# Scores and states of the second batch: two separate steps in the gaps between MLP units, in place of one block inside a unit's output products

## The chip, the cores and the metric

One core of a Trainium2 chip runs the whole kernel. The metric is the device time of one execution in microseconds. The kernel before took 1019.85 us (median of three runs, 1019.58 to 1019.98).

## The reference

All tensors are fp32. A retention layer without softmax (8 batches, 8 heads, 576 tokens, head size 64) is followed by a two-layer MLP over 4608 tokens, with a leaky ReLU of a learned slope for each of the 2048 hidden channels:

```python
scores = scale * np.matmul(q, k.transpose(0, 1, 3, 2))
gamma = 1.0 - 2.0 ** (-5.0 - np.arange(H, dtype=np.float32))
Dmat = np.where(rel >= 0, gamma[:, None, None] ** rel[None, :, :], 0.0)
ret = np.matmul(scores * Dmat[None, :, :, :], v)

h = x @ w_in                                  # x: (4608, 512), w_in: (512, 2048)
g = np.maximum(h, 0.0) + alpha * np.minimum(h, 0.0)
return g @ w_out                              # w_out: (2048, 512)
```

## The kernel before

**Attention in chunks.** Two heads make a pair; each batch has four pairs, numbered through, so the second batch is pairs 4 to 7. From the second batch on, a pair is worked in nine chunks of 64 tokens. Four things happen to it:

- its operands are prepared: `scale_pair` (step "p": GpSimd scales `qx` in L534, ScalarE scales `vn` in L539) and `transposes` (step "t": two 32x32 block transposes on VectorE, L545);
- scores of each chunk, `k q^T`, by 18 small matmuls, which VectorE scales and masks into `mt`, while ScalarE copies `qT` into the other half of `mt`;
- states of the first eight chunks, `k^T v`, by 16 small matmuls, which `running_sums` (step "u") adds up with the decay: one ScalarE copy (L556), then six VectorE instructions (L558, L562, L564); `pair_sums` (step "w", L570) copies the sums to `vn` on ScalarE;
- values (step "v"): 36 small matmuls of `vn` with `mt` (L630), ScalarE copies of the result into the MLP's input `xb` (L641), and the loads of the pair after next on SP's queue.

**The MLP.** From the third block of 256 tokens on (`mlp_unit`), each unit of 2 x 128 hidden channels is a Strassen-like product with seven multiplications instead of eight, from combined weights. The first two blocks (`PLAIN`) use plain products while the weights are still arriving. A plain unit is `plain_unit` (8 instructions, in the trace 16 matmuls of 256 columns, into `ph`, L429, then two ScalarE activations, L433 and L435), `plain_relu` (two VectorE instructions, L445, that read `ph` and make `g`), and one unit later `mlp_out`, which calls `plain_out` (4 instructions, in the trace 8 matmuls of 512 columns, L408). `ph` lies in one PSUM bank with the tag `psh0`, of which there is one, so a unit's first matmul follows the relu of the unit before. The names `ps`, `pu` and `pv` are tiles of the tag `psa`, of which there are two.

**Weights.** Each piece of a weight (512 KB) is loaded into a ring, split by ScalarE (`piece_in`, L299 and L301) and rounded by three VectorE instructions (`piece_out`, L310, L313, L315) and one of GpSimd (L317), which also fetches the piece six ahead. `combine` makes the weights' sums on GpSimd (L327).

**The order.** The part up to `ordered.close()` is written out by hand: each engine executes in the order in which the program calls. Every engine runs its own instructions in order and waits for the others by semaphores. The change acts on the last loop of this part: twelve plain units, here unit 0 to unit 11, with at most two pieces in each. The steps of pairs 4 to 7 are hung into it by two tables, `before` (behind the relu, ahead of the products) and `after` (behind the products and the second `piece_in`). Pair n's scores and states come together in `pair_front`: `amid` is called from within `mlp_out`, ahead of its last product, in units 2, 4, 7 and 9. The ninth chunk's scores have a PSUM tile of their own there, `pe`, with the tag `psh0`, and the masks of that chunk are two VectorE instructions (L607), beside four of 256 columns (L614). The other eight chunks share two `psa` tiles with the states.

```python
        if n in fronts:
            mlp_out((3, lambda: amid(fronts[n])))
            piece_out(1)
        else:
            piece_out(1)
            mlp_out()
```

After the loop the blocks of the other batches follow, with `joint` doing the attention of pairs 8 to 31 between the MLP units; there values and scores share tiles, and `pair_front` stays in use.

Of the kernel before, what the change touches and what calls it, by code (L numbers as in the profile page):

```python
# [18 lines left out]
def kernel(  # L19
# [380 lines left out]
    def plain_out(kb, i, g, between):  # L400
        if i == 0:
            acc[kb] = [ps_o.tile([P, DM], FP32, tag=f"pso{2 * kb + m}", name=f"po{m}_{kb}")
                       for m in range(2)]
        for x in range(2):
            for m in range(2):
                if between and 2 * x + m == between[0]:
                    between[1]()
                nc.tensor.matmul(acc[kb][m], g[:, 2 * x + m],  # L408
                                 w_out[i][:, 2 * x:2 * x + 2].rearrange("p x f -> p (x f)"),
                                 start=(i == 0 and x == 0), stop=(i == NU - 1 and x == 1))  # L410
        if i == NU - 1:
            po = acc.pop(kb)
            osb = ring.tile([P, 2, DM], FP32, tag=f"o{kb}", name=f"osb_{kb}")
            for m in range(2):
                t0 = kb * TB + m * P
                nc.scalar.copy(osb[:, m], po[m])
                nc.sync.dma_start(out[t0:t0 + P, :], osb[:, m])
        if kb == PLAIN[-1] and i % UST == UST - 1:
            waiting.extend((w_in[i // UST], x) for x in S_WORK)
            waiting.extend((w_out[j], x) for j in range(i + 1 - UST, i + 1) for x in T_WORK)  # L420
# [127 lines left out]
    def chunk(j):  # L548
        return slice(j * C, (j + 1) * C)

    def running_sums(n, even, odd):
        c = pairs[n][1]
        su = attn.tile([P, S], FP32, tag="kT", name=f"su_{n}")[:, 0:S - D].rearrange(
            "p (j d) -> p j d", d=D)
        g1, g2 = gch[:, 0, c:c + 1], gch[:, 1, c:c + 1]
        nc.scalar.copy(su[:, 0::2], even)  # L556
        for h2 in range(2):
            nc.vector.scalar_tensor_tensor(  # L558
                out=su[half(h2), 1::2], in0=su[half(h2), 0::2], scalar=g1[half(h2)],
                in1=odd[half(1 - h2)], op0=ALU.mult, op1=ALU.add)  # L560
        for j in range(3, NJ - 1, 2):
            nc.vector.scalar_tensor_tensor(out=su[:, j], in0=su[:, j - 2], scalar=g2,  # L562
                                           in1=su[:, j], op0=ALU.mult, op1=ALU.add)
        nc.vector.scalar_tensor_tensor(out=su[:, 2::2], in0=su[:, 1:NJ - 3:2], scalar=g1,  # L564
                                       in1=even[:, 1:], op0=ALU.mult, op1=ALU.add)
        return su
# [4 lines left out]

    later = []

    def last_chunk(n, extra):
        kT, qT = turned[n]
        for h2 in range(2):  # L580
            nc.tensor.matmul(extra[half(1 - h2)], kT[half(h2), chunk(NJ - 1)],  # L581
                             qT[half(h2), chunk(NJ - 1)], start=True, stop=True)

    def pair_front(n, kT, qT, kn, vn, extra):

        c = pairs[n][1]
        mts[n] = mt = attn.tile([P, 2 * S], FP32, tag="at", name=f"mt_{n}").rearrange(
            "p (h j s) -> p h j s", h=2, s=C)
        assert C == D and NJ == 9
        ps = [ps_tile([P, 2, NM - 1, C], f"ps{p2}_{n}") for p2 in range(2)]  # L590
        for j in range(NJ - 1):
            for h2 in range(2):
                x = half((1 - h2, h2)[j % 2])
                nc.tensor.matmul(ps[j % 2][x, 0, j // 2],  # L594
                                 kT[half(h2), chunk(j)], qT[half(h2), chunk(j)],
                                 start=True, stop=True, skip_group_check=True)
        for j in range(NJ - 1):
            for h2 in range(2):
                x = half((h2, 1 - h2)[j % 2])
                nc.tensor.matmul(ps[j % 2][x, 1, j // 2], kn[half(1 - h2), j],  # L600
                                 vn[half(1 - h2), h2, j], start=True, stop=True,
                                 skip_group_check=True)
        for h2 in range(2):
            nc.scalar.copy(mt[half(h2), h2].rearrange("p j s -> p (j s)"), qT[half(h2)])
        for h2 in range(2):
            to = half(1 - h2)
            nc.vector.scalar_tensor_tensor(  # L607
                out=mt[to, h2, NJ - 1], in0=extra[to],
                scalar=th[to, 3, 2 * c + h2:2 * c + h2 + 1], in1=mask(to),
                op0=ALU.mult, op1=ALU.mult)  # L610
        for p2 in range(2):
            for h2 in range(2):
                h, to, x = 2 * c + h2, half(1 - h2), (1 - h2, h2)[p2]
                nc.vector.scalar_tensor_tensor(  # L614
                    out=mt[to, h2, p2:NJ - 1:2], in0=ps[p2][half(x), 0],
                    scalar=th[to, 3, h:h + 1],
                    in1=mask(to)[:, None, :].to_broadcast([C, NM - 1, C]),
                    op0=ALU.mult, op1=ALU.mult)
        later.append(lambda: running_sums(n, ps[0][:, 1], ps[1][:, 1]))

    def pair_values(n, vn, mt, pv=None, then=None):
        b, c = pairs[n]
# [214 lines left out]
    part_scale(1, 2)  # L837
    part_transposes(1, 0)
    piece_in(1)
    mlp_out((2, lambda: part_transposes(1, 1)))  # L840
    piece_out(1)
    piece_in(1)
    banks = part_scores(1)
# [38 lines left out]
    def step(what, n):  # L882
        if what == "p":
            scale_pair(n)
        elif what == "t":
            if n > last:
                combine_x(len(PLAIN))
            turned[n] = transposes(n)
        elif what == "u":
            sus[n] = later.pop(0)()  # L890
        elif what == "w":
            pair_sums(loaded[n][3], sus.pop(n))
        elif what == "v":
            pair_values(n, loaded[n][3], mts[n])
            del loaded[n]
            loaded[n + 2] = load_pair(n + 2)

    def amid(n):  # L900
        extra = ps_h.tile([P, C], FP32, tag="psh0", name=f"pe_{n}")
        last_chunk(n, extra)
        pair_front(n, *turned.pop(n), loaded[n][0], loaded[n][3], extra)

    last = 2 * NPAIR - 1
    before, after, fronts = {1: (("t", NPAIR),)}, {0: (("p", NPAIR),)}, {}
    for n, at in zip(range(NPAIR, last + 1), (2, 4, 7, 9)):
        fronts[at] = n  # L910
        after[at] = (("u", n),)
        before[at + 1] = (("w", n), ("p", n + 1))
        after[at + 1] = (("v", n), ("t", n + 1))

    units = [(kb, i) for i in range(UST, NU) for kb in PLAIN]
    for n, (kb, i) in enumerate(units):
        plain_unit(kb, i)
        plain_relu()
        for x in before.pop(n, ()):
            step(*x)  # L920
        piece_in(1)
        if n in fronts:
            mlp_out((3, lambda: amid(fronts[n])))
            piece_out(1)
        else:
            piece_out(1)
            mlp_out()
        combine(1)
        piece_in(1)
        for x in after.pop(n, ()):  # L930
            step(*x)
        piece_out(1)
        combine(2)
    assert not before and not after
    ordered.close()
    tc.no_sync_barrier()
    enqueue(0)
# [8 lines left out]
    def joint(n):  # L946
        pv = [ps_h.tile([P, 8, C], FP32, tag=f"psh{m}", name=f"pv{m}_{n}") for m in range(2)]


        extra = pv[1][:, 7]  # L950

        def chunk_8():
            if n < len(pairs):
                last_chunk(n, extra)

        if n - 1 in mts:
            pair_values(n - 1, loaded.pop(n - 1)[3], mts.pop(n - 1), pv, chunk_8)
        else:
            chunk_8()
        if n == len(pairs):  # L960
            return
        pair_front(n, *turned.pop(n), loaded[n][0], loaded[n][3], extra)
        if n + 1 < len(pairs):
            if n + 1 not in loaded:
                loaded[n + 1] = load_pair(n + 1)
            later.append(lambda: operands(n + 1))
# [3 lines left out]
    for b in range(2, B):  # L970


        nq = len(queue)
        at = [u + (u % NU == 0) for u in (c * nq // NPAIR + 2 for c in range(NPAIR))]
        if b == 2:
            at = [0, 3] + at[1:]
        for u in range(nq):
            first = queue[0][1] == 0
            pop_units(1)
            if later and not first:  # L980
                su = later.pop(0)()
                if su is not None:
                    pair_sums(loaded[n - 1][3], su)
            if u in at:
                assert not later
                joint(n)
                n += 1
        enqueue(b)
# [32 lines left out]
```

## Time and profile before

| | |
|---|---|
| median of three runs | 1019.85 us |
| time of the profiled execution | 1019.85 us |
| span of the profiled execution, first to last instruction | 1018.1 us |
| granted TensorE clock, mean | 0.999 |
| busy: PE, PEld, DVE, ACT, POOL | 1002.7, 898.6, 774.0, 266.2, 179.7 us |
| the twelve plain units of the loop | from 60.67 to 161.21 us |

PE is TensorE's matmul, PEld its weight load, DVE is VectorE, ACT ScalarE, POOL GpSimd, SP the engine that issues most of the loads. Times within the profile count from the first instruction. The ends of matmuls are modelled, so the start of the next instruction is the better mark of when PE went on. In a line of the timeline the columns are start, duration, engine, source line, operation, tiles and shapes; a bracket behind it gives the idle time of the engine ahead of it and what ended it. In the table of waits they are the total, the number of waits and the longest, in us. Matmuls in fp32 appear twice in the trace for one instruction of the program.

### The profile page before, as it was taken

What the parts mean: (1) busy time and instruction counts of PE and PEld (TensorE: products, weight loads), DVE (VectorE), ACT (ScalarE), POOL (GpSimd) and SP (SyncE); (2) the same over time, 40 slices, a digit from 0 to 9 for tenths busy, and PEclk for the clock granted to TensorE, in tenths of its full rate; (3) what the DMA queues carried; (4) which work ended last, traced back from release to release, by engine and by line L of the source; (5) the groups of instructions that cost most, each with busy time, mean ns of one, the idle gap of its engine ahead of it and who ended that gap; (6) DMA issues with size and microseconds to landing.
All of it is one profiled execution on the core that took longest, in us unless ns stands there. A gap on an engine that the chain in (4) does not pass through costs nothing.

```text
span 1018.1 us, 22392 instructions
## 1 busy us (share of the span) xinstructions
PE 1002.7 (98%) x9023; PEld 898.6 (88%) x9023; DVE 774.0 (76%) x2094; ACT 266.2 (26%) x602; POOL 179.7 (18%) x200
## 2 busy tenths in 40 slices
PE   7999999999999999999999999999999999999998
PEld 6766667999999999999999999999999999999997
DVE  6668895987787878786877787877778786667665
ACT  4556654222222222021121222222222210000000
POOL 5646664400100020100001000200020001010000
PEclk9999999999999999999999999999999999999999
DMA  9964754332232323121220232322222000000000
GB/s 242 246 176 123 170 104 100 61 73 54 42 69 39 66 48 69 18 53 34 51 47 23 46 69 48 69 48 63 54 42 51 14 22 1 22 1 22 1 22 22
DMA packets 229592, 64.25 MB, mean 63 GB/s; under 512 B 214368, under 2 KB 223088, under 8 KB 229488
## 3 DMA queue, kind: packets, MB, share of 16 engines
q1 hardware_dynamic: 227088, 62.02, 27.0%
q8 instruction: 71, 1.16, 0.5%
q10 hardware_dynamic: 2400, 0.79, 0.4%
q14 instruction: 33, 0.27, 0.1%
HBM read 53.35 MB, written 9.44 MB: 62 GB/s over the span
## 4 chain that ended last, share of the span: by engine, by line
PE 84%; DVE 0%; ACT 0%; DVEq 0%; issue 0%; ACTq 0%
PE ph L473 40%; PE po L391 38%; PE pv L630 3%; PE ps L594 1%; PE ps L600 1%; PE po L408 1%; PE pv L581 1%; PE ph L429 0%; ACT vn L570 0%; DVE s L370 0%; DVE u L370 0%; DVE osb L371 0%; DVEq L1016 0%; DVE osb L370 0%; ACTq L570 0%
## 5 line engine op out<-in xcount | busy, mean ns | idle before, releaser
L391 PE MATMUL po<-w_out,g 128*128 128x256 f32 x1792 | 408.1, 379 | 0.0
L391 PEld LDWEIGHTS po<-w_out,g 128*128 128x128 f32 x1792 | 330.7, 190 | 39.7
L484 DVE TENSOR_TENSOR g<-ph,g 128x256 f32<-128x256 f32 (+1 forms) x512 | 187.6, 387 | 136.4 <-PE ph L473 68.5
L473 PE MATMUL ph<-xb,w_in 128*128 128x128 f32 x2048 | 272.7, 276 | 0.0
L473 PEld LDWEIGHTS ph<-xb,w_in 128*128 128x128 f32 x2048 | 257.1, 192 | 7.4 <-issue 0.5
L473 PE MATMUL ph<-xt,w_in 128*128 128x128 f32 x1536 | 213.3, 275 | 0.0
L473 PEld LDWEIGHTS ph<-xt,w_in 128*128 128x128 f32 x1536 | 192.1, 192 | 0.0
L479 ACT COPY g<-ph 128x128 f32<-128x128 f32 x128 | 34.0, 265 | 404.1 <-PE ph L473 391.7
L495 DVE TENSOR_TENSOR g<-g 128x128 f32<-128x128 f32 x512 | 127.9, 291 | 7.0
L534 POOL TENSOR_TENSOR qx<-qx,tabx 128x576 f32<-128x576 f32 x28 | 32.8, 1170 | 355.1 <-DMA qx<-in_q_dram 276.5
L489 DVE SCALAR_TENSOR_TENSOR g<-g 128x512 f32<-128x512 f32 x128 | 90.0, 703 | 3.1
L487 DVE TENSOR_SCALAR g<-g,alpha 128x256 f32<-128x256 f32 x256 | 85.0, 374 | 3.6
L429 PE MATMUL ph<-xb,w_in 128*128 128x256 f32 x256 | 58.4, 382 | 2.1 <-DVE g L445 2.1
L408 PE MATMUL po<-w_out,g 128*128 128x512 f32 x128 | 59.1, 598 | 0.9 <-DVE g L445 0.9
L429 PEld LDWEIGHTS ph<-xb,w_in 128*128 128x128 f32 x256 | 48.0, 190 | 12.7 <-issue 4.0
L614 DVE SCALAR_TENSOR_TENSOR mt<-ps,th,mask 64x256 f32<-64x256 f32 x112 | 54.1, 483 | 3.9 <-PE ps L600 1.5
L641 ACT COPY xb<-pv 128x256 f32<-128x256 f32 (+3 forms) x84 | 23.1, 315 | 126.5 <-PE pv L630 126.5
L570 ACT COPY vn<-su 64x512 f32<-64x512 f32 x56 | 34.5, 617 | 80.1 <-DVE su L564 79.7
L459 POOL TENSOR_TENSOR xt<-xb 128x256 f32<-128x256 f32 x16 | 11.7, 728 | 196.5 <-PE ph L473 196.5
L607 DVE SCALAR_TENSOR_TENSOR mt<-pv,th,mask 64x64 f32<-64x64 f32 x48 | 13.6, 283 | 40.0 <-ACT xb L641 39.7
L630 PEld LDWEIGHTS pv<-mt,vn 128*64 128x64 f32 x1008 | 32.6, 138 | 12.9 <-DVE g L495 7.6
L539 ACT ACTIVATE vn<-vn,tabv 64x576 f32<-64x576 f32 x56 | 43.3, 772 | 1.7 <-DMA vn<-in_v_dram 0.5
(129 smaller groups left out, 742.6 us busy)
## 6 DMA issues: line engine op xcount, KB each, us to landing
out_dram<-osb SPq DMA_DIRECT2D x34, 256.0 KB, 2.1
kx<-in_k_dram SPq DMA_DIRECT2D x112, 72.0 KB, 2.7
qx<-in_q_dram SPq DMA_DIRECT2D x112, 72.0 KB, 2.9
vn<-in_v_dram SPq DMA_DIRECT2D x56, 144.0 KB, 3.4
kn<-in_k_dram SPq DMA_DIRECT2D x56, 144.0 KB, 3.7
raw<-in_moe_w_in_dram SPq DMA_DIRECT2D x24, 256.0 KB, 4.0
raw<-in_moe_w_out_dram SPq DMA_DIRECT2D x10, 512.0 KB, 5.1
w_in<-in_moe_w_out_dram SPq DMA_DIRECT2D x6, 512.0 KB, 4.6
```

Source lines behind the costliest of these rows:

```text
L391: nc.tensor.matmul(acc[kb][n // 2][:, n % 2, :], g[:, x, :], w_out[i][:, y, :], start=(i == 0 and n % 2 == 0), stop=(i == NU - 1 and (n % ...
L408: nc.tensor.matmul(acc[kb][m], g[:, 2 * x + m], w_out[i][:, 2 * x:2 * x + 2].rearrange("p x f -> p (x f)"), start=(i == 0 and x == 0), sto ...
L429: nc.tensor.matmul(ph[:, x], w_in[i // UST][:, cc // 2 * 2 + x, i % UST, cc % 2], xb[kb][:, cc], start=(cc == 0 and x == 0), stop=(cc == N ...
L473: nc.tensor.matmul(ph[m][:, o], w_in[i // UST][:, l, i % UST, cc], r[:, cc], start=(n in (0, 3) and cc == 0), stop=(n in (2, 6) and cc == ...
L484: nc.vector.tensor_tensor(out=o, in0=x0, in1=x1, op=ALU.add)
L487: nc.vector.tensor_scalar(g[:, 4 + 2 * m:6 + 2 * m], g[:, 2 * m:2 * m + 2], 0.0, alpha[:, fc:fc + 1], ALU.min, ALU.mult)
L489: nc.vector.scalar_tensor_tensor(out=g[:, 0:4].rearrange("p x t -> p (x t)"), in0=g[:, 0:4].rearrange("p x t -> p (x t)"), scalar=0.0, in1 ...
L495: ins = nc.vector.tensor_tensor(out=g[:, o, :], in0=g[:, x0, :], in1=g[:, x1, :], op=op)
L539: nc.scalar.activation(vn[x, h2], vn[x, h2], ACTF.Copy, scale=tabv[x, c:c + 1])
L570: nc.scalar.copy(vn[half(h2), h2, 1:], su[half(h2)])
L614: nc.vector.scalar_tensor_tensor(out=mt[to, h2, p2:NJ - 1:2], in0=ps[p2][half(x), 0], scalar=th[to, 3, h:h + 1], in1=mask(to)[:, None, :]. ...
L630: nc.tensor.matmul(pv[j >= j1][half(h2), j - (j1 if j >= j1 else 0)], vn[:, h2, j], mt[:, h2, j], start=True, stop=True)
```

## The change

The block of scores and states is taken out of the middle of the output products, and becomes two steps of their own, "s" (`pair_scores`) and "u" (`pair_states`, which ends with the running sums). All nine chunks' scores go to two `psa` tiles of up to five chunks, so `pe` and its two mask instructions go, and the four masks cover nine chunks (two of 320 columns, two of 256). States have two `psa` tiles of their own. The steps are worked off from one list, one entry in each gap; from unit 2 on a unit has two gaps, A behind the relu and ahead of the products, B behind the products and the second `piece_in`:

| pair | scores | states and sums | sums to `vn`, next pair's scaling | values, next pair's transposes |
|---|---|---|---|---|
| 4, before | 2, inside products | 2 (sums in B) | 3 A | 3 B |
| 4, after | 2 A | 2 B | 3 A | 3 B |
| 5, before | 4, inside products | 4 (sums in B) | 5 A | 5 B |
| 5, after | 4 B | 5 A | 5 B | 6 A |
| 6, before | 7, inside products | 7 (sums in B) | 8 A | 8 B |
| 6, after | 7 A | 7 B | 8 A | 8 B |
| 7, before | 9, inside products | 9 (sums in B) | 10 A | 10 B |
| 7, after | 9 B | 10 A | 10 B | 11 A |

The third step ("w", "p") is in gap A before, and in pairs 5 and 7 in gap B after. The combination of the third block's input, `combine_x(2)`, moves with the transposes of pair 8. In unit 0 the scaling of pair 4 moves ahead of the second piece. The number of matmuls stays; VectorE has eight instructions fewer. Code outside the loop is the same but for a few lines that pass the running sums on, and its order stays.

```diff
+    def pair_scores(n, kT, qT):
+        c = pairs[n][1]
+        mt = attn.tile([P, 2 * S], FP32, tag="at", name=f"mt_{n}").rearrange(
+            "p (h j s) -> p h j s", h=2, s=C)
+        ps = [ps_tile([P, NM, C], f"ps{p2}_{n}") for p2 in range(2)]
+        for j in range(NJ):
+            for h2 in range(2):
+                x = (1 - h2, h2)[j % 2]
+                nc.tensor.matmul(ps[j % 2][half(x), j // 2], kT[half(h2), chunk(j)],
+                                 qT[half(h2), chunk(j)], start=True, stop=True)
+        for h2 in range(2):
+            nc.scalar.copy(mt[half(h2), h2].rearrange("p j s -> p (j s)"), qT[half(h2)])
+        for p2 in range(2):
+            for h2 in range(2):
+                h, to, x = 2 * c + h2, half(1 - h2), (1 - h2, h2)[p2]
+                nm = NM - p2
+                nc.vector.scalar_tensor_tensor(
+                    out=mt[to, h2, p2::2], in0=ps[p2][half(x), 0:nm], scalar=th[to, 3, h:h + 1],
+                    in1=mask(to)[:, None, :].to_broadcast([C, nm, C]), op0=ALU.mult, op1=ALU.mult)
+        return mt
+
+    def pair_states(n, kn, vn):
+        ps = [ps_tile([P, NM - 1, D], f"pu{p2}_{n}") for p2 in range(2)]
+        for j in range(NJ - 1):
+            for h2 in range(2):
+                x = (h2, 1 - h2)[j % 2]
+                nc.tensor.matmul(ps[j % 2][half(x), j // 2], kn[half(1 - h2), j],
+                                 vn[half(1 - h2), h2, j], start=True, stop=True)
+        return running_sums(n, *ps)
...
     def step(what, n):
...
+        elif what == "s":
+            mts[n] = pair_scores(n, *turned.pop(n))
         elif what == "u":
-            sus[n] = later.pop(0)()
+            sus[n] = pair_states(n, loaded[n][0], loaded[n][3])
...
-    def amid(n):
-        extra = ps_h.tile([P, C], FP32, tag="psh0", name=f"pe_{n}")
-        last_chunk(n, extra)
-        pair_front(n, *turned.pop(n), loaded[n][0], loaded[n][3], extra)
-
     last = 2 * NPAIR - 1
-    before, after, fronts = {1: (("t", NPAIR),)}, {0: (("p", NPAIR),)}, {}
-    for n, at in zip(range(NPAIR, last + 1), (2, 4, 7, 9)):
-        fronts[at] = n
-        after[at] = (("u", n),)
-        before[at + 1] = (("w", n), ("p", n + 1))
-        after[at + 1] = (("v", n), ("t", n + 1))
+    steps = [(("t", NPAIR),)]
+    for n in range(NPAIR, last + 1):
+        steps += [(("s", n),), (("u", n),), (("w", n), ("p", n + 1)), (("v", n), ("t", n + 1)), ()]
+
+    def gap():
+        for x in steps.pop(0) if steps else ():
+            if x == ("t", last + 1):
+                combine_x(len(PLAIN))
+            step(*x)
...
         plain_unit(kb, i)
         plain_relu()
-        for x in before.pop(n, ()):
-            step(*x)
+        if n >= 1:
+            gap()
         piece_in(1)
-        if n in fronts:
-            mlp_out((3, lambda: amid(fronts[n])))
-            piece_out(1)
-        else:
-            piece_out(1)
-            mlp_out()
+        piece_out(1)
+        mlp_out()
+        if n == 0:
+            step("p", NPAIR)
         combine(1)
         piece_in(1)
-        for x in after.pop(n, ()):
-            step(*x)
+        if n >= 2:
+            gap()
         piece_out(1)
         combine(2)
```

## The prediction

> **What bounds the kernel now.** I read the page first, then busy time by stretches, the waits of TensorE, and the timelines of PE and DVE where the change acts. The page's engine row:
>
> ```profile
> PE 1002.7 (98%) x9023; PEld 898.6 (88%) x9023; DVE 774.0 (76%) x2094; ACT 266.2 (26%) x602; POOL 179.7 (18%) x200
> ```
>
> PE is busy for 98% of the span, so a change pays only where PE idles. The twelve plain units of the loop run from 60.67 (first `ph`, L429) to 161.21 (first L473). The stretches are units 0-1, 2-6, 7-11 and the rest:
>
> ```profile
> 60.67:74.44 13.77, 13.77 (x49) 9.12 (x48) 7.07 (x12) 8.14 (x14) 7.20 (x6) 1.00 0.77 185
> 74.44:118.35 43.91, 41.19 (x329) 27.30 (x328) 38.09 (x70) 27.97 (x55) 27.71 (x27) 1.00 0.51 142
> 118.35:161.21 42.86, 41.09 (x329) 27.55 (x330) 32.08 (x59) 22.50 (x45) 31.12 (x35) 1.00 0.57 114
> ```
>
> After the range come its length and the busy time of PE, PEld, DVE, ACT and POOL. Units 0-1 have no idle PE: 6.885 us a unit. In units 2-11 PE idles 2.72 + 1.77 = 4.49 us, with DVE at 38.09 of 43.91. Behind 161.21 PE waits for nothing that the trace lists. What PE waits for inside:
>
> ```profile
> PE ph L429 <- DVE g L445: 2.1, 4, 0.8
> PE pe L581 <- DVE g L445: 1.3, 2, 0.7
> PE pv L630 <- ACT vn L570: 1.0, 3, 0.4
> ```
>
> So a unit's `ph` (or the `pe` tile, in the same PSUM buffer) waits for DVE's late relu of the unit before. Pair 4, PE and then DVE:
>
> ```profile
> 74.44 3.62 PE L429 MATMUL ph<-xb,w_in 128*128 128x256 f32 x16
> 77.90 2.74 PE L408 MATMUL po<-w_out,g 128*128 128x512 f32 x6
> 80.56 0.27 PE L581 MATMUL pe<-qT,kT 64*64 64x64 f32 x2
> ...
> 81.76 1.13 PE L408 MATMUL po<-w_out,g 128*128 128x512 f32 x2
> 82.72 3.62 PE L429 MATMUL ph<-xb,w_in 128*128 128x256 f32 x16
> 86.17 3.60 PE L408 MATMUL po<-w_out,g 128*128 128x512 f32 x8
> 89.70 1.61 PE L630 MATMUL pv<-mt,vn 128*64 128x64 f32 x36
> 91.75 3.69 PE L429 MATMUL ph<-xb,w_in 128*128 128x256 f32 x16 [0.45 <-DVE g L445]
> ```
>
> ```profile
> 79.22 0.87 DVE L445 SCALAR_TENSOR_TENSOR g<-g,nalpha,ph 128x256 f32<-128x256 f32 x2 [0.36 <-ACT ph L435]
> 80.94 0.58 DVE L607 SCALAR_TENSOR_TENSOR mt<-pe,th,mask 64x64 f32<-64x64 f32 x2 [0.86 <-PE pe L581]
> 81.89 1.99 DVE L614 SCALAR_TENSOR_TENSOR mt<-ps,th,mask 64x256 f32<-64x256 f32 x4 [0.36 <-PE ps L600]
> 83.80 0.68 DVE L310 TENSOR_SCALAR wc<-wa 128x512 f32<-128x512 f32 x1
> ...
> 85.97 0.98 DVE L558 SCALAR_TENSOR_TENSOR su<-su,gch,ps 64x256 f32<-64x256 f32 x2
> ...
> 88.68 0.69 DVE L310 TENSOR_SCALAR wc<-wa 128x512 f32<-128x512 f32 x1
> ...
> 90.74 0.86 DVE L445 SCALAR_TENSOR_TENSOR g<-g,nalpha,ph 128x256 f32<-128x256 f32 x2
> ```
>
> DVE stands still 1.2 us for the front, which PE reaches only after six of eight `po` matmuls. Masks, a weight piece, running sums and a second piece follow in order. The next relu starts at 90.74 though ACT had finished near 87.5, and `ph` starts 1.01 us after the relu's start.
>
> **The change, part by part.** (a) *Scores leave the middle of the products.* For pairs 4 and 6 they stand before `mlp_out`, straight after `ph`, so they are ready (77.90 + 0.75) before the relu ends (80.0). DVE's 0.86 and 0.36 go. (b) *Six mask instructions become four.* The chunk 8 mask (283 ns, twice) goes; two of four grow from 256 to 320 columns, which no row shows. It costs at least the 256-column row, 483 ns, at most that plus a 64-column row, 766; the line through both rows gives 550, nearest to the 256 row, which I take. A mask set is 2 x 0.55 + 2 x 0.48 = 2.05 us, where relu's end to piece took 83.80 - 80.0 = 3.8: DVE is 1.75 earlier. Between the bounds, 1.9 to 1.3.
>
> (c) *Pairs 5 and 7 are spread.* Scores go after unit 4's products, states after unit 5's `ph`, values after unit 6's `ph`, not after unit 5's products (7 likewise in 9 to 11). The relu of unit 5 then has only a mask set and a piece ahead of it, and sums fall behind it. (d) *`pe` goes*, and with it its wait for the relu.
>
> Walk units 2-6 with rows of the trace: relu 0.8, a piece 2.06 (88.68 to 90.74), sums 2.7 (85.97 to 88.68), transposes 1.35, `ph` 3.45, products 3.45. Masks end at 82.05, piece 84.1, sums 86.8, piece 88.9: relu 3 runs 88.9-89.7. PE: scores to 78.65, products to 82.1, states to 82.9, `ph` 3 from 83.0, products to 89.95, values to 91.35. `ph` 4 can start then; relu 3 was done 1.6 earlier. DVE next waits for ACT, which copies the sums (1.26) and scales the next values (1.57) before its own part of a piece: piece 91.0-93.1, transposes 94.4, piece 96.5, relu 4 to 97.3. `ph` 5 comes at 99.0: 1.7 spare. Relu 5 (from 103.8) is on time for `ph` 6 at 106.6; its sums end at 107.3, ACT's copies at 108.6, values at 110.05; relu 6 ends at 112.2 for `ph` 7 at 114.9. So no relu is late by this walk, and the wait on ACT in `pv` goes also.
>
> What is late next: the states' matmuls of pairs 4 and 6 take the two `psa` banks, so they wait for the masks' end: 82.05 + 0.14 against 82.1, about 0.1 each. Behind them on PE stands the whole next unit, so this counts in full.
>
> Queues: SP takes pair 7's twelve loads behind one more 512 KB piece, about 1.04 us of issue. By the walk they start near 115 and take some 7.5 us to issue (117.09 to 124.6 in this trace); the scaling of pair 7 comes near 129. On POOL `qx`'s scaling moves past one or two sums (0.73 to 1.3 us); the transposes meet it with less than 0.5 us to wait. With both covers gone, DVE's transposes would come some 2 us later, beside 1.6 us spare. ACT's scaling of pair 4 goes ahead of a piece in unit 0, where DVE idles 1.69 behind it: nothing.
>
> PE's own cost: splitting the front adds two boundaries a pair between 128-row products and 64-row blocks. Six products at the pitch of 0.43 end at 80.48, `pe` starts at 80.56: 0.08; behind the front two products take 0.96, not 0.87: 0.09. Four pairs x 2 x 0.1 = 0.8 us. The Trainium skill, "TensorEngine Tiling (Array Packing)", Key Properties, speaks against the split: a change of tiling mode drains TensorE. It gives no price, and the 0.08 agrees with it.
>
> L562 varies from 285 to 1186 ns; three took 1.46 in one pair and 2.36 in another. Were every set as slow, relu 3 would come 0.9 later, still inside 1.6. "SBUF — State Buffer", Who interferes with whom, states that a DVE instruction with two SBUF inputs is blocked whole by a GpSimd one that reads SBUF. Taken at its word, an estimate from that page is that each of the three loses a whole POOL row of 1.26, 3.8 a set; a relu would come 2.2 late in four pairs, and the sum would be 1023.2. The rows decide for 0.9.
>
> The sum. Stalls listed on `ph` and `pe`: 2.1 + 1.3 = 3.4. `pv`: from its first start to its end it took 1.61, 2.15, 1.61 and 2.5; the undisturbed block at 187.70 takes 1.27, so 7.87 - 5.08 = 2.8. Together 6.2, less 0.8 and 0.2: 5.2. From the other side: units 2-11 bare are 10 x 6.885, four pairs with scores and states at 1.6 and values at 1.4, and 0.2: 81.05, against 86.77: 5.7. I take 5.5. The profiled execution took 1019.85, 1.75 beyond its span and equal to the median: 1019.85 - 5.5 = 1014.35.
>
> **The rivals.** *Only half goes.* The margins are 1.6 and 1.7 us; a piece of 2.26 (66.23 to 68.49) in place of 2.06, a loaded ACT and slow L562 use them up, and a `ph` still waits in each pair. Half of 5.5: 1017.1. For it: DVE has 36.9 us of work in 40.5.
>
> *The seam takes it back.* Values 7, `combine_x(2)` and the transposes of pair 8 now come a whole `ph` (3.45) later, and the first L473 follows one set of products after. If POOL (four operations, 2.8 us) or the loads of pair 9, which wait for values 7, are late by that, the gain is 2: 1017.8. Against: POOL had finished its four at 157.0, 4 us ahead.
>
> *Nothing moves*, if the DVE backlog meets PE later anyway: 1019.8. Against: behind 161.21 the trace lists no wait of PE.
>
> *Slower.* In place of the relu, PE waits at L580 for the masks. If DVE comes to the masks D late, pairs 4 and 6 pay D + 0.1, pairs 5 and 7, with a `ph` between, D - 0.8: 4D - 1.4. Without the freed gain (the relus stay late too) that passes 2 us at D = 0.85; at D = 2.06, one piece, it is 6.8: 1026.7. It needs a lateness that the walk does not show in either half.
>
> **How the numbers follow.** Forecast 0.63, half 0.14, seam 0.07, nothing 0.06, slower 0.10. The low end has all 6.2 to 6.7 us of stalls gone without the boundaries: 1013.1. The high end takes in half and seam: 1017.9. 0.2% is 2.04 us, about what a measurement of this kernel can tell. Faster: forecast, half and seam, 0.84; same 0.06; slower 0.10.
>
> **What would show it.** Right: first L473 near 155.7; no wait of `ph` on L445 in units 3 to 11; masks right behind relu 2; PE waits at the states' matmuls of 0.1 to 0.3. Wrong: `ph` still waiting for L445, states waiting more than 0.5 for masks, or an idle PE at the first L473.

## The result, and the profile after

The changed kernel takes 1014.62 us (median of four runs, 1014.25 to 1014.94), the kernel before 1019.91 us in its runs beside it: a ratio of 0.9949, 95% interval 0.9931 to 0.9966. That is 5.29 us less, where 5.5 was forecast. The profiled execution shown here took 1014.25 us, with a span of 1012.5.

The page's engine row:

```profile
PE 1001.5 (99%) x9023; PEld 897.3 (89%) x9023; DVE 772.4 (76%) x2086; ACT 266.6 (26%) x602; POOL 180.0 (18%) x200
```

PE's share rises by one point, its busy time falls by 1.2 us, its instructions stay; DVE has eight instructions fewer. Busy time by stretches, from the first `ph` of unit 2 on (columns as before):

```profile
74.09:114.81 40.72, 40.72 (x329) 27.00 (x328) 37.51 (x66) 27.30 (x55) 27.98 (x27) 1.00 0.57 159
114.81:155.53 40.72, 40.72 (x329) 27.00 (x328) 30.97 (x55) 22.84 (x46) 28.95 (x32) 1.00 0.57 110
155.53:1012.50 856.97, 853.01 (x7881) 794.12 (x7879) 654.64 (x1854) 176.82 (x429) 82.07 (x98) 1.00 0.20 43
```

Both halves now take 40.72 us, and PE is busy in all of it; before they took 43.91 and 42.86 with 2.72 and 1.77 idle. The rest takes 856.97, before 856.89. So the gain lies in units 2 to 11, and nothing is given back later: 86.77 us became 81.44. All waits of PE that the trace still lists in the whole span:

```profile
PE pt L698 <- DMA w_out<-in_k_dram: 5.8, 2, 4.8
PE po L408 <- DVE g L445: 0.9, 1, 0.9
```

Both lie ahead of unit 0. Pair 4, PE:

```profile
74.09 3.62 PE L429 MATMUL ph<-xb,w_in 128*128 128x256 f32 x16
77.64 0.80 PE L562 MATMUL ps<-qT,kT 64*64 64x64 f32 x36
78.36 3.70 PE L408 MATMUL po<-w_out,g 128*128 128x512 f32 x8
81.99 0.69 PE L580 MATMUL pu<-vn,kn 64*64 64x64 f32 x32
82.62 3.72 PE L429 MATMUL ph<-xb,w_in 128*128 128x256 f32 x16
86.18 3.60 PE L408 MATMUL po<-w_out,g 128*128 128x512 f32 x8
89.70 1.27 PE L655 MATMUL pv<-mt,vn 128*64 128x64 f32 x36
90.90 3.72 PE L429 MATMUL ph<-xb,w_in 128*128 128x256 f32 x16
```

and DVE:

```profile
78.86 0.87 DVE L445 SCALAR_TENSOR_TENSOR g<-g,nalpha,ph 128x256 f32<-128x256 f32 x2 [0.37 <-ACT ph L435]
79.77 2.13 DVE L570 SCALAR_TENSOR_TENSOR mt<-ps,th,mask 64x320 f32<-64x320 f32 x4
81.82 0.68 DVE L310 TENSOR_SCALAR wc<-wa 128x512 f32<-128x512 f32 x1
...
88.76 0.86 DVE L445 SCALAR_TENSOR_TENSOR g<-g,nalpha,ph 128x256 f32<-128x256 f32 x2
```

The masks follow the relu without a bracket, that is without a wait, and the piece behind them starts 2.05 us after them. The next relu starts 9.90 us behind this one; before it was 90.74 - 79.22 = 11.52. Values take 1.27 us, no longer 1.61.

**How the experiments are compared.** Some experiments move less than the medians can tell apart. Two parts of the trace give a finer measure. From the first L473 to the end every kernel here takes 856.88 to 857.07 us. The first `ph` of unit 2 starts anywhere from 72.92 to 75.38, in two runs of the very same changed kernel at 74.09 and 72.92, so the part ahead of it carries most of the spread between executions. What lies between is the stage that the change acts on; in those two runs it took 81.44 and 81.45 us. The "stage" below is this length, from one profiled execution each; a median is of the runs named.

### The profile page after: what moved, and what is told of

Read it like the earlier page. It is cut to its first block, busy times and chain, and to the rows that moved or that the text cites. A ratio compares the mean times of both kernels' runs of the same rounds, so it can differ in the third digit from the quotient of the medians.

```text
span 1012.5 us, 22397 instructions
## 1 busy us (share of the span) xinstructions
PE 1001.5 (99%) x9023; PEld 897.3 (89%) x9023; DVE 772.4 (76%) x2086; ACT 266.6 (26%) x602; POOL 180.0 (18%) x200
## 4 chain that ended last, share of the span: by engine, by line
PE 98%; DMA 1%; POOL 0%; DVE 0%; ACT 0%; issue 0%; ACTq 0%; DVEq 0%; POOLq 0%
PE ph L473 40%; PE po L391 38%; PE ph L429 6%; PE po L408 6%; PE pv L655 3%; PE ps L619 1%; PE ps L625 1%; DMA w_out<-in_q_dram 1%; PE pv L975 1%; PE ps L719 1%; PE pv L772 0%; PE pv L781 0%; PE ps L562 0%; PE idle L849 0%; POOL pa L732 0%; PE pu L580 0%
## 5 line engine op out<-in xcount | busy, mean ns | idle before, releaser
L391 PEld LDWEIGHTS po<-w_out,g 128*128 128x128 f32 x1792 | 330.6, 190 | 39.8 <-DVE osb L370 0.2
L473 PE MATMUL ph<-xb,w_in 128*128 128x128 f32 x2048 | 272.7, 276 | 0.0
L473 PEld LDWEIGHTS ph<-xb,w_in 128*128 128x128 f32 x2048 | 257.1, 192 | 7.4 <-issue 0.5
L473 PE MATMUL ph<-xt,w_in 128*128 128x128 f32 x1536 | 213.3, 275 | 0.0
L473 PEld LDWEIGHTS ph<-xt,w_in 128*128 128x128 f32 x1536 | 192.1, 192 | 0.0
L639 DVE SCALAR_TENSOR_TENSOR mt<-ps,th,mask 64x256 f32<-64x256 f32 x96 | 46.4, 483 | 2.2
L408 PEld LDWEIGHTS po<-w_out,g 128*128 128x128 f32 x128 | 23.4, 190 | 24.5 <-issue 21.8
```

The lines of the kernel that those rows point to most:

```text
L391: nc.tensor.matmul(acc[kb][n // 2][:, n % 2, :], g[:, x, :], w_out[i][:, y, :], start=(i == 0 and n % 2 == 0), stop=(i == NU - 1 and (n % ...
L408: nc.tensor.matmul(acc[kb][m], g[:, 2 * x + m], w_out[i][:, 2 * x:2 * x + 2].rearrange("p x f -> p (x f)"), start=(i == 0 and x == 0), sto ...
L473: nc.tensor.matmul(ph[m][:, o], w_in[i // UST][:, l, i % UST, cc], r[:, cc], start=(n in (0, 3) and cc == 0), stop=(n in (2, 6) and cc == ...
L639: nc.vector.scalar_tensor_tensor(out=mt[to, h2, p2:NJ - 1:2], in0=ps[p2][half(x), 0], scalar=th[to, 3, h:h + 1], in1=mask(to)[:, None, :]. ...
```

## The experiments

All were timed with the kernel before beside them on the same chip (1019.34 us with the first three and the four idle instructions, 1019.49 with the three that start from the kernel before, 1019.45 with `hybrid`, its neighbour `after_again` and the two idle instructions).

### From the changed kernel: undo one part

**The spreading of pairs 5 and 7 undone** (`a_no_spread`):

```diff
-        steps += [(("s", n),), (("u", n),), (("w", n), ("p", n + 1)), (("v", n), ("t", n + 1)), ()]
+        steps += [(("s", n),), (("u", n),), (("w", n), ("p", n + 1)), (("v", n), ("t", n + 1))]
+        if n % 2:
+            steps += [(), ()]
```

> The changed kernel with pairs 5 and 7 placed as pairs 4 and 6 are (scores in gap A of units 4 and 9, states in gap B of the same unit, sums to vn and scaling in gap A of the next unit, values in its gap B). Theory (the gain comes from masks that follow the relu without a wait, and from no pe): 0.2 us of wait at the states of pairs 5 and 7 and relus still just on time, 1014.6 to 1015.2 us. Rival (the spreading of pairs 5 and 7 carries the gain): half of the gain goes, 1017 us or more, with waits of ph on L445 back in units 5, 6, 10 and 11.

Measured: 1015.07 us (five runs), ratio to before 0.9957 (0.9945 to 0.9969); stage 82.64, which is 1.2 more than 81.44. PE, the states of pair 5 and the `ph` of unit 7:

```profile
98.20 1.03 PE L580 MATMUL pu<-vn,kn 64*64 64x64 f32 x32
...
114.90 3.69 PE L429 MATMUL ph<-xb,w_in 128*128 128x256 f32 x16 [0.30 <-DVE g L445]
```

The states take 0.34 longer than the 0.69 of the changed kernel (they wait for the masks inside), in pairs 5 and 7 alike, and one relu is late. The spreading is worth about a fifth of the gain, not half. The 0.2 a pair that was expected was too small.

**Six masks in a set again** (`a_six_masks`): the ninth chunk is masked by two instructions of its own, behind the other four.

```diff
-                nm = NM - p2
+                nm = NM - 1
-                    out=mt[to, h2, p2::2], in0=ps[p2][half(x), 0:nm], scalar=th[to, 3, h:h + 1],
+                    out=mt[to, h2, p2:NJ - 1:2], in0=ps[p2][half(x), 0:nm],
+                    scalar=th[to, 3, h:h + 1],
...
+        for h2 in range(2):
+            h, to, x = 2 * c + h2, half(1 - h2), 1 - h2
+            nc.vector.scalar_tensor_tensor(
+                out=mt[to, h2, NJ - 1], in0=ps[0][half(x), NM - 1], scalar=th[to, 3, h:h + 1],
+                in1=mask(to), op0=ALU.mult, op1=ALU.mult)
```

> The changed kernel with the masks of the ninth chunk as two VectorE instructions of their own again, six in a set in place of four (2.5 us in place of 2.05). Theory: the states of pairs 4 and 6 come 0.45 us later each, pairs 5 and 7 have a ph between and hide it: 1014.62 + 0.9 = 1015.5 us. Rival (fewer VectorE instructions are the gain): 1.75 us a pair come back, 1018 us or more.

Measured: 1015.37 us (five runs), ratio 0.996 (0.9948 to 0.9972); stage 82.25, 0.81 more. PE at pair 4's states, then `ph`:

```profile
81.89 1.10 PE L586 MATMUL pu<-vn,kn 64*64 64x64 f32 x32
82.92 3.72 PE L429 MATMUL ph<-xb,w_in 128*128 128x256 f32 x16
```

1.03 us lie between the two starts, in the changed kernel 0.63: 0.4 in each of two pairs. The set itself takes 2.51 us from its start to the next instruction's, 0.46 more than 2.05; pairs 5 and 7, with a `ph` between scores and states, lose nothing. Most of the rest of the 1.75 a pair was VectorE's waits for the scores (1.2), and these do not come back here.

**Scores back inside the products** (`a_scores_inside`): all else as in the changed kernel, with pairs 5 and 7 placed as before.

```diff
+        if n in inside:
+            mlp_out((3, lambda: step("s", inside[n])))
+            piece_out(1)
+        else:
+            piece_out(1)
+            mlp_out()
```

> The changed kernel with the scores of every pair back ahead of the last output product, in units 2, 4, 7 and 9 (states in gap B of the same unit, the rest as in the kernel before); pe stays away and the masks stay four. Theory: VectorE waits about 1.2 us for the scores, states wait 1.2 us for the masks, 1.3 us a pair: 1014.62 + 5.2 = 1019.8 us, most of the change's gain lost. Rival (the gain is the tile pe or the two mask instructions, not the place of the scores): 1015 to 1016 us.

Measured: 1019.33 us (eleven runs), ratio 1.0 (0.9991 to 1.0008); stage 86.94, 5.5 more than the changed kernel. As the spreading is undone here too, the place by itself is the difference to `a_no_spread` (82.64): 4.3. The first masks on DVE, and PE's waits in the stage:

```profile
80.22 2.13 DVE L570 SCALAR_TENSOR_TENSOR mt<-ps,th,mask 64x320 f32<-64x320 f32 x4 [1.32 <-PE ps L562]
```

```profile
PE pu L580 <- DVE mt L570: 2.5, 4, 0.6
PE pu L580 <- issue: 0.8, 4, 0.2
PE ph L429 <- DVE g L445: 0.3, 1, 0.3
```

DVE waits 1.32 us for the scores, and PE then waits for the masks: in this form fewer masks and no `pe` gain nothing while the scores stay where they were.

### From the kernel before: do one part

**Only another bank for `pe`** (`b_pe_bank`):

```diff
-        extra = ps_h.tile([P, C], FP32, tag="psh0", name=f"pe_{n}")
+        extra = ps_h.tile([P, C], FP32, tag="psh1", name=f"pe_{n}")
```

> The kernel before with pe in the PSUM buffer of the weight conversion (psh1) in place of that of ph (psh0); all else, the place of the front too, as before. Theory: only pairs 5 and 7 had PE waiting for the relu at pe (0.63 and 0.70 us); that goes and the late relus behind come about 0.6 earlier: 1019.9 - 1.3 = 1018.6 us. Rival (pe is the main cause): 1016 us or less.

Measured: 1017.28 us (eleven runs), ratio 0.9981 (0.9973 to 0.999); stage 85.30, 1.47 less than before.

```profile
PE ph L429 <- DVE g L445: 2.1, 4, 0.9
PE pv L630 <- ACT vn L570: 1.0, 3, 0.4
```

The waits of `pe` (1.3) are gone from the list; those of `ph` and `pv` stand as they were. The relus do come earlier, as was expected: that of unit 5 starts 34.22 us after unit 2's `ph`, before 34.93. But PE reaches the next `ph` earlier by as much, so its waits stay.

**Only the place** (`b_front_early`): the whole front ahead of the first product, `pe` last in it.

```diff
-            mlp_out((3, lambda: amid(fronts[n])))
+            mlp_out((0, lambda: amid(fronts[n])))
```

> The kernel before with the whole front (scores, states and, last, the ninth chunk's scores) ahead of the first output product instead of the last, pe still in the buffer of ph. Theory: VectorE gets its masks earlier, but PE waits about 1.1 us a pair at pe for the relu of the same unit: 1017 to 1018.5 us, between the two kernels. Rival (the place inside the products costs nothing): 1020 us or more.

Measured: 1019.12 us (eleven runs), ratio 0.9996 (0.9987 to 1.0005); stage 86.57, 0.2 less. A miss: no gain was found.

```profile
PE pe L581 <- DVE g L445: 5.1, 4, 1.5
PE ph L429 <- DVE g L445: 0.3, 1, 0.3
```

The waits of `ph` fall from 2.1 to 0.3, and `pe` takes them over: 1.08 us in pairs 4 and 6, 1.47 in 5 and 7, where 1.1 was reckoned for all. A wait was moved, not removed.

**Both** (`b_front_early_bank`): the two edits above together.

> As the front moved ahead of the first output product, and pe in psh1 too. Theory: masks follow the relu, pe waits only for the end of the piece ahead of the relu (nothing in pairs 4 and 6, about 0.5 us in 5 and 7), and no block is split, which saves two boundaries of 0.1 a pair: 1015 to 1015.8 us, nearly the whole gain without splitting scores and states. Rival (the split or the spreading is needed): 1017.5 us or more.

Measured: 1015.37 us (five runs), ratio 0.9965 (0.9951 to 0.9979); stage 83.23, 3.54 less.

```profile
PE pe L581 <- DVE w_in L315: 0.7, 1, 0.7
PE pe L581 <- DVE w_out L315: 0.7, 1, 0.7
PE ph L429 <- DVE g L445: 0.6, 1, 0.6
```

Alone the two edits are worth 1.47 and 0.2, together 3.54: the place pays only when `pe` no longer hangs on the relu of the same unit. Two thirds of the gain come without splitting the block. What is left are waits of pairs 5 and 7, where the weight piece that holds psh1 ends late, and unit 7's `ph`.

### The best of both

**`hybrid`**, beside the unaltered kernel on the same chip (`after_again`): pairs 4 and 6 as one early block, pairs 5 and 7 in separate, spread steps.

```diff
+        elif what == "s" and n % 2 == 0:
+            extra = ps_h.tile([P, C], FP32, tag="psh1", name=f"pe_{n}")
+            pair_front(n, *turned.pop(n), loaded[n][0], loaded[n][3], extra, True)
         elif what == "s":
             mts[n] = pair_scores(n, *turned.pop(n))
+        elif what == "u" and n % 2 == 0:
+            sus[n] = later.pop(0)()
```

> The changed kernel unaltered, beside the next one on the same chip: 1014.6 us, and 81.4 us from the first ph of unit 2 to the first L473.

> The changed kernel, but with pairs 4 and 6 as one block of scores and states in gap A of units 2 and 7 (pe in psh1, its matmuls last), and pairs 5 and 7 in separate, spread steps. Theory (no relu is late in either form, so only the blocks' boundaries are left): two boundaries of about 0.1 us and one wait of 0.1 us for the masks less in two pairs, 16.46 in place of 16.8 us for units 2 and 3: 80.8 us for the stage, 1014 us. Rival (the longer set of six masks makes a relu late): 82 us for the stage or more.

Measured: `after_again` 1013.45 us (five runs, 1013.0 to 1014.18), ratio 0.9946 (0.9932 to 0.996), stage 81.45; that is 6.0 us under the kernel before in the runs beside it. `hybrid` 1013.51 us (five runs, 1012.7 to 1014.84), ratio 0.9945 (0.9932 to 0.9957). By the medians the two are equal. The stage of `hybrid`:

```profile
75.38:156.20 80.82, 80.82 (x658) 54.08 (x657) 69.88 (x124) 49.95 (x100) 56.63 (x58) 1.00 0.57 135
```

80.82 us, as expected, without idle PE: 0.62 less. Two boundaries fewer in each of two pairs account for 0.4; the rest is the block, which takes 1.20 and 1.28 us in one piece, where scores and states apart take 0.72 and 0.63. Its profiled execution reached unit 2 at 75.38, the latest of all. The shorter stage is shown in one profile; a shorter time is not.

### What a late mask costs

**Idle work ahead of the masks**, four instructions (`a_masks_late`) or two (`a_masks_late_half`):

```diff
+        for _ in range(4):
+            nc.vector.tensor_scalar(spare, spare, 1.0, None, ALU.mult)
```

> The changed kernel with four idle VectorE instructions of 128x256 on a spare tile (about 1.4 us) ahead of each set of masks. Theory: pairs 4 and 6 pay nearly the whole 1.4 at the states, pairs 5 and 7 about 0.4 to 0.6: 1018.2 to 1019 us, with PE waits at L580 that name the masks. Rival (VectorE has over 2 us to spare there): under 1015.5 us.

> The changed kernel with two idle VectorE instructions ahead of each set of masks; by the run with four, which took 2.5 to 3.3 us, they take 1.2 to 1.6 us. Theory (the lateness D counts by itself, and the granted clock falls only where PE stands for about 2 us): pairs 4 and 6 pay D + 0.1, pairs 5 and 7 D - 0.8 or so, 3.5 to 4.5 us in all, 1018 to 1019.2 us, with no slower ph behind the waits. Rival (any wait at the states slows the matmuls behind it): 1021 us or more.

Measured with two: 1017.8 us (eleven runs), ratio 0.9986 (0.9978 to 0.9995); stage 85.40, 3.96 more. The delay, pair 4:

```profile
78.63 1.39 DVE L569 TENSOR_SCALAR spare<-spare 128x256 f32<-128x256 f32 x2
80.04 2.13 DVE L574 SCALAR_TENSOR_TENSOR mt<-ps,th,mask 64x320 f32<-64x320 f32 x4
```

The median lies just under the 1018 us expected, the stage within the 3.5 to 4.5. Counted from the `ph` ahead of them, the masks of the four pairs start 1.29, 1.56, 1.57 and 1.46 us later than in the changed kernel. PE loses 1.23, 0.48, 1.52 and 0.41 at their states, and 0.32 at pair 5's values. The prediction's 4D - 1.4 gives 4.5 for these four D.

With four: 1027.38 us (six runs, 1025.01 to 1031.21), ratio 1.0084 (1.0067 to 1.0101); the profiled execution is the slowest of the six, and its stage took 98.07, 16.6 more. A miss twice over. The four instructions took 2.53 us in pair 4, 3.26 in pair 5 and up to 4.13 in pair 7, not 1.4. And the matmuls behind the long waits ran slower, which no theory had. Pair 4's states and the `ph` behind them:

```profile
83.83 0.33 PE L584 MATMUL pu<-vn,kn 64*64 64x64 f32 x4 [1.35 <-issue]
84.79 1.05 PE L584 MATMUL pu<-vn,kn 64*64 64x64 f32 x28 [0.63 <-DVE mt L574]
85.77 4.96 PE L431 MATMUL ph<-xb,w_in 128*128 128x256 f32 x16
```

That `ph` and the products of unit 5 as stretches; the last columns are the granted clock, the DMA share and GB/s:

```profile
85.77:90.57 4.80, 4.80 (x18) 4.07 (x17) 4.58 (x10) 0.30 (x1) 1.96 (x2) 0.73 0.30 90
...
109.47:113.01 3.54, 3.54 (x13) 1.63 (x10) 3.42 (x7) 2.75 (x5) 2.02 (x2) 1.00 0.78 261
```

## Why the prediction was right

**The bound.** The change pays where PE idles, and only there: the stage lost 5.33 us (5.5 forecast), the part behind it moved by 0.08. By the medians the gain is 5.3 us in the first comparison and 6.0 in the second, so that the first came as near to 5.5 as it did is partly luck; the stage is the firmer figure, and lies between the prediction's two sums, 5.2 and 5.7.

**(a) and (d), place and `pe`.** The masks follow the relu at once, relu 3 started 9.9 us behind relu 2 (the walk: 9.7), no `ph` and no `pv` waits. `a_scores_inside` takes the place away and loses 4.3 by it, 5.5 with the spreading; `b_front_early_bank` does place and bank alone and gains 3.54. Neither the place (0.2) nor the bank (1.47) alone does it, which the walk had not said: it had the relus' lateness and `pe` as two separate terms.

**(b), masks.** The set took 2.05 us, the value that was chosen between 1.9 and 2.5; a mask of 320 columns takes 549 ns, where 550 was read off a line through two other rows. Undone, it costs 0.81.

**(c), the spreading.** The step held in its direction; undone it costs 1.2.

**The new wait.** Forecast 0.1 at the states of pairs 4 and 6, and this did not come; the sign "PE waits at the states' matmuls of 0.1 to 0.3" did not show. Pair 5 has the rows to compare with:

```profile
94.46 3.60 PE L408 MATMUL po<-w_out,g 128*128 128x512 f32 x8
97.98 0.80 PE L562 MATMUL ps<-qT,kT 64*64 64x64 f32 x36
98.71 3.72 PE L429 MATMUL ph<-xb,w_in 128*128 128x256 f32 x16
102.36 0.69 PE L580 MATMUL pu<-vn,kn 64*64 64x64 f32 x32
102.99 3.70 PE L408 MATMUL po<-w_out,g 128*128 128x512 f32 x8
```

Products alone take 3.43 us (63.77 to 67.20), ahead of a block 97.98 - 94.46 = 3.52, behind one 106.53 - 102.99 = 3.54, and between two, ahead of pair 4's states, 81.99 - 78.36 = 3.63. The two boundaries make up all of it. In `a_six_masks` masks that end 0.46 later delay these states by 0.4, so here they were ready about 0.05 us ahead.

**The boundaries.** `ph` takes 3.45 us between products, 3.56 behind a block (82.62 to 86.18) and 3.65 between two (98.71 to 102.36): about 0.1 a boundary, as taken from 0.08 and 0.09. Ten bare units are 68.85 us and the four pairs' blocks took 81.44 - 68.85 = 12.6, 3.15 a pair, where 3.05 was reckoned. This is the 0.4 between the stage's 81.05 and 81.44. The term that was too small is scores and states at 1.6: with four boundaries they take 0.72 + 0.63 + 0.4 = 1.75, while values take the 1.4 reckoned. In one block, as before and in `hybrid`, scores and states take 1.20; so the split costs up to 0.15 a pair beside its boundaries, which the first sum left out. The rule of the Trainium skill, "TensorEngine Tiling (Array Packing)", Key Properties, that a change of tiling mode drains TensorE, agrees with these 0.1 us.

**The slow L562.** Under its new line, L595, three took 1.47 us in pair 4 and at most 2.22, in pair 5, inside the spare that the walk left. The larger loss that the prediction worked out from "SBUF — State Buffer", Who interferes with whom, was not seen: no relu was late.

**The rivals.** *Half goes* would have shown waits of `ph`; there are none. *Nothing moves* lies outside the interval of the ratio. *The seam*: GpSimd ends the four operations of `combine_x(2)` at 154.9, the first L473 starts at 155.53 without a wait, so this held with 0.6 us to spare, not with the several us that the earlier trace had. *Slower*: its condition did not hold. With two idle instructions its formula gives 4.5 where 3.96 was measured; the shape is right, nearly D in pairs 4 and 6, but pairs 5 and 7 hid 1.1 us, not 0.8. With four, D is 2.4 to 4.0 us, and it gives 10.9 where 16.6 was measured, because the matmuls slowed as well.

## What to carry to other kernels

A block that another engine waits for belongs where its inputs are first ready, and its output tile must not share a buffer with anything that hangs on a later step: here the two together gained 3.54 us, alone 0.2 and 1.47. Where the engine in question is the bound only for a stage, sum the waits on that stage and walk the in-order queues through it; with the part ahead of it and the part behind it left out, its length in two profiles of one kernel agreed within 0.01 us, so changes of 0.5 us can still be compared.

## What the runs showed of the hardware

With four idle instructions, PE stood at the states' matmuls for 1.98 us (1.35 and 0.63, with four short matmuls between) in pair 4, 1.69 in pair 5, 2.2 in pair 6 and 2.57 in pair 7, all in the one execution that was profiled. Behind 1.69 us the granted clock stayed at 1.00. Behind the three others it was 0.73, 0.67 and 0.57 on average in the next stretch, and 3.56 us of `ph` became 4.80 and 5.22, 3.54 us of products 6.14. So these three waits cost not only themselves but 1.2 to 2.6 us more.

The averages hide two values. In short stretches the clock reads 1.00 or 0.50, and it is 0.50 for 3.41, 3.41 and 6.83 us, from 84.92, 132.70 and 156.60 on: 14 and 7 times 3.41 us lie between these starts. Windows of this length ahead of each fall, the one of pair 5 without a fall, and what followed the first and the last (columns as before):

```profile
81.50:84.92 3.42, 1.43 (x14) 0.50 (x16) 3.31 (x7) 1.39 (x3) 0.62 (x1) 1.00 0.44 153
84.92:88.33 3.41, 3.41 (x34) 2.84 (x35) 3.22 (x7) 0.37 (x1) 1.40 (x2) 0.50 0.02 5
105.39:108.81 3.42, 1.77 (x11) 1.16 (x9) 3.31 (x7) 1.08 (x2) 0.79 (x1) 1.00 0.92 176
129.29:132.70 3.41, 1.21 (x33) 0.77 (x32) 3.27 (x8) 0.72 (x2) 0.14 (x1) 1.00 0.84 176
153.18:156.60 3.42, 1.34 (x9) 0.78 (x7) 3.31 (x6) 1.08 (x2) 3.26 (x5) 1.00 0.00 0
156.60:160.01 3.41, 2.91 (x30) 1.77 (x31) 2.78 (x6) 0.37 (x1) 3.41 (x5) 0.50 0.00 0
```

PE was busy for 42, 35 and 39% of the windows ahead of the three falls, and for 52% of pair 5's. A full window at 0.50 brought the clock back, one with 85% (the last line) did not. In the stages of all other runs, cut in the same way, no window is under 57% (`b_front_early`, 138.41 to 141.82, with a wait of 1.47 us), and the clock stayed at 1.00. In these runs, then, the clock goes with the busy share of such a window rather than with the length of one wait; where between 42 and 52% the limit lies, and whether it holds elsewhere, is not shown. The Trainium skill, "TensorE: Matmul & The Clock Gate", Part 1, names an idle window of about 3.4 us for the fall to half the clock; the length agrees, but here PE was not idle for a whole window.
